# Cached grouped-query attention with a token mixer: half of wq of two heads on partitions 0 to 63, loaded as transfers of four DMA engines

## The chip, the core and the metric

One core of one Trainium2 chip runs the kernel. The metric is device time in microseconds (us), from the start to the end of one execution of the program. Before the change it was 2498.15 us (median of 3 runs, 2498.01 to 2498.72).

## What is computed

Two layers run one after the other on a single new token of two sequences (B = 2, D = 512). Each layer is a block of attention over a cache, and then a token mixer. There are 32 query heads in 8 groups; a group of four shares one head of keys and values, of 32768 positions by 128. Both layers use the same caches and weights. All of it is float32.

```python
def _A_ref(x, k_cache, v_cache, wq, wo):
    q = (x @ wq).reshape(B, Sq, 32, 128).transpose(0, 2, 1, 3)
    k = repeat(k_cache, 4, axis=1)
    v = repeat(v_cache, 4, axis=1)
    p = softmax(einsum("bhqd,bhkd->bhqk", q, k) * 128 ** -0.5)
    o = einsum("bhqk,bhkd->bhqd", p, v)
    return o.transpose(0, 2, 1, 3).reshape(B, Sq, 4096) @ wo
...
x = x + _A_ref(layernorm(x), k_cache, v_cache, wq, wo)
x = x + _B_ref(layernorm(x), w1, b1, w2, b2)
x = x + _A_ref(layernorm(x), k_cache, v_cache, wq, wo)
x = x + _B_ref(layernorm(x), w1, b1, w2, b2)
```

`_B_ref` is a small network (1792 hidden units) across the one token, for each of the 512 channels.

## The kernel before, in words

**Units.** The work is cut into units (layer, b, h): one sequence and one head of keys and values. A unit reads its keys (64 groups of 512 columns, 16 MB) and then its values (64 groups, 16 MB). `k_step` (L350 to L370) multiplies four groups of keys by the four queries into a tile `scores`; `v_step` (L418 to L440) multiplies four groups of values by the exponentials into `acc`. Each such call is a step, and `Order` (L44) lists all steps in the order in which TensorE takes them: the keys of one unit, then the values of the unit before. At the change of layer a few units of both layers are interleaved, since the last sums of the first layer must be complete before a query of the second can be made.

**Memory.** All that is read from DRAM lands in one tile, `mem`, of 106 cells; a cell is 512 floats on 128 partitions (256 KB). `plan_loads` (L120) decides ahead of time, in the order of need, in which cells each load goes and after which step (`begun`) its cells are free. A load is 32 cells (8 MB) of keys or values in most of the run, and smaller around the change of layer and at the end; a piece of weights, wq or wo of one head, is 4 cells (`WCELLS`, 1 MB). There are 240 loads in all. Ten of the cells are left beside three loads of 32, and in most of the run wq of the coming head lies in cells 0 to 3 and wo of the present one in cells 4 to 7.

**Queues.** All these loads are issued by SyncE (the SP queue) in the order of the plan, by `load` (L893): weights at L899, keys and values at L904. The queue is in order: a load that waits for its cells holds back all that come behind it. A transfer of 128 partitions runs on all 16 DMA engines of the core, and each engine works through its own part of the loads in their order. ScalarE issues the two small inputs and the first result.

**Queries.** For each head, `make_q` (L309) forms the queries of both sequences: `wide_products` (L321) multiplies the normalized input by wq. D = 512 lies as four tiles of 128 on the partitions: `xw` (128 x 4 x 32) holds the input, and wq of a head is seen as 128 x 4 x 512. Tile d gives a product of 128 rows into the 32 partitions from 32 d of a tile `bcast` (L325), and `narrow_products` (L332) sums the four and turns them. The tile `xw` is written at the start (`first_input`, L301) and by `change_0` and `change_2` at the change of layer.

Of the kernel before, what the change touches and what calls it, by code (L numbers as in the profile page):

```python
# [8 lines left out]
F32 = mybir.dt.float32  # L9
# [4 lines left out]
P = 128  # L14
G = 512
# [5 lines left out]
WCELLS = 4  # L21
# [17 lines left out]
STEP_US = 1.6  # L39
ASK_Q = 16  # L40
ASK_O = 8


class Order:  # L44
# [75 lines left out]
def plan_loads(order, weights, busy):  # L120
# [13 lines left out]
    queue, array, begun, i = 2.0, 0.0, -1, 0  # L134
# [10 lines left out]
    while i < len(asked) or weights:  # L145
        if weights and (i == len(asked) or weights[0][0] <= asked[i][0]):
            _, name, last = weights.pop(0)
            label, sizes, stays = ("W", name, 0), (WCELLS,), True
        else:
            _, kind, u, g = asked[i]  # L150
            label, stays = (kind, u, g), (kind, u, g) in order.kept
            n = 1
            while (
                i + n < len(asked)
                and asked[i + n][1:] == (kind, u, g + n)
                and (g + n) % HALF
                and ((kind, u, g + n) in order.kept) == stays
            ):
                n += 1
            sizes = [s for s in SIZES if s <= n] or [n]  # L160
            if label in order.sizes:
                sizes = [min(order.sizes[label], n)]
        best = None
        for s in sizes:
            spots = range(CELLS - s + 1)
            found = None
            for a in spots if stays else reversed(spots):
                t = ready(range(a, a + s))
                if t is not None:
                    wait = max(0.0, t + LEAD_US - queue)  # L170
                    key = (wait, t if s == max(SIZES) or label[:2] == ("V", order.last) else 0.0)
                    if found is None or key < found[3]:
                        found = (wait, s, a, key)
            if found is not None and (best is None or found[0] < best[0] - 0.01):
                best = found
            if best is not None and best[0] == 0.0:
                break
        wait, s, a, _ = best
        begun = max(begun, *(last_use[a : a + s]))
        loads.append((label, s, a, begun))  # L180
        queue += wait + s * CELL_US + LOAD_US
        if label[0] == "W":
            last_use[a : a + s] = [last] * s
        else:
            for j in range(s):
                key = (kind, u, g + j)
                for k in (key, order.kept.get(key)):
                    if k is not None:
                        landed[k] = queue + LAND_US
                        last_use[a + j] = step_of[order.back.get(k, k)]  # L190
                if key in order.held:
                    landed[order.held[key]] = queue + LAND_US
            i += s
        while len(done) < len(steps):
            kind, u, g = steps[len(done)]
            keys = [(kind, u, g + j) for j in range(STEP)]
            if any(k not in landed for k in keys):
                break
            array = max(array, *(landed[k] for k in keys)) + STEP_US
            array += busy.get(len(done), 0.0)  # L200
            done.append(array)
# [1 line left out]


@with_exitstack
def gqa_mixer_kernel(ctx: ExitStack, tc: tile.TileContext, x, kt, v, wqo, cols, out):
    nc = tc.nc
    B, D = out.shape
    HKV = wqo.shape[0]
# [2 lines left out]
    DT = D // P  # L212
# [7 lines left out]
    const = ctx.enter_context(tc.tile_pool(name="const", bufs=1))  # L220
# [10 lines left out]
    def cells(a, n):  # L231
        return mem[:, a * G : (a + n) * G]
# [20 lines left out]
    misc = pfix.tile([P, G], F32, name="misc")  # L253
    S = [const.tile([P, G], F32, name=f"S{k}") for k in range(2)]
    xw = const.tile([P, DT, 32], F32, name="xw")
    RAW = B
    xT = {}
    turn = [0, 0, 0]
# [23 lines left out]
    def first_input():  # L282
# [16 lines left out]
        for b in range(B):  # L299
            xT[b] = xcols[:, b, :]  # L300
            nc.vector.tensor_scalar_mul(xw[:, :, b], cen[:, b, :], rs[:, b : b + 1])  # L301

    def row_tile():
        return work.tile([P, D], F32, name="row", bufs=1)

    wq_sb, wo_sb = {}, {}
# [14 lines left out]
    def wide_products(us, wq):  # L321

        q_ps[us] = pfix.tile([P, G], F32, name="bcast")
        for d in range(DT):
            nc.tensor.matmul(q_ps[us][32 * d : 32 * d + 32, :], xw[:, d, :], wq[:, d, :], start=True, stop=True)  # L325

    def narrow_products(us, side):

# [452 lines left out]
    def at(p, f, *args, us=0.0):  # L781
        hooks.setdefault(p, []).append((f, args))
        busy[p] = busy.get(p, 0.0) + us
# [32 lines left out]
    for u in order.units:  # L816
# [35 lines left out]
        e = v_end  # L852
# [24 lines left out]
        at(e + 3, unread, u, G)  # L877
        at(e + 4, change_3, y, us=1.0)
        at(e + 4, unread, u, G // 2)
        assert e + 4 < first["K", y]  # L880

    for x, _, y in order.changes:
# [10 lines left out]
    def load(label, n, a):  # L893
        kind, u, g = label
        if kind == "W":
            part, layer, h = u
            w = D * R
            at_w = 0 if part == "q" else w
            nc.sync.dma_start(cells(a, n), wqo[h][:, at_w : at_w + w])  # L899
            (wq_sb if part == "q" else wo_sb)[layer, h] = cells(a, n).rearrange("p (t c) -> p t c", t=DT)  # L900
            return
        layer, b, h = u
        src = (kt if kind == "K" else v)[b * HKV + h, g // HALF, :, (g % HALF) * G : (g % HALF + n) * G]
        nc.sync.dma_start(cells(a, n), src)  # L904
        for j in range(n):
            at_cell[kind, u, g + j] = a + j
            if (kind, u, g + j) in order.kept:
                at_cell[order.kept[kind, u, g + j]] = a + j
# [6 lines left out]
        load(label, n, a)  # L915
    constants()
    first_input()
    for step in range(3):
        make_q(opening_q, step)
    for p, (kind, u, g) in enumerate(steps):  # L920
# [8 lines left out]
def _layout(A_x, A_k_cache, A_v_cache, A_wq, A_wo, B_w1, B_b1, B_w2, B_b2):  # L929
    import numpy as np  # L930

    B, HKV, SK, DH = A_k_cache.shape
    D = A_x.shape[-1]
    U = B * HKV
    kt = A_k_cache.reshape(U, 2, NG, 32, 2, 2, 8, 2, 2, DH).transpose(0, 1, 9, 4, 7, 8, 2, 5, 6, 3)
    wq = A_wq.reshape(D // P, P, HKV, -1).transpose(2, 1, 0, 3)
    wo = A_wo.reshape(HKV, -1, DH, D).transpose(0, 2, 1, 3)
    w1, b1, w2 = (a.reshape(P, -1) for a in (B_w1, B_b1, B_w2))
    none = np.zeros_like(w2)
    w2z = np.stack([none, w2], axis=2).reshape(P, -1)  # L940
    cols = [w1, b1, w2z, none[:, :1], np.broadcast_to(B_b2.reshape(1, 1), (P, 1))]
    return {
        "x": np.ascontiguousarray(A_x.reshape(B * (D // P), P).T),
        "kt": np.ascontiguousarray(kt).reshape(U, 2, DH, HALF * G),
        "v": A_v_cache.reshape(U, 2, P, HALF * G),
        "wqo": np.concatenate([wq.reshape(HKV, P, -1), wo.reshape(HKV, DH, -1)], axis=2),
        "cols": np.concatenate(cols, axis=1),
    }


_INS = ["x", "kt", "v", "wqo", "cols"]


# [20 lines left out]
```

## Time and profile before

| | |
|---|---|
| median of the runs | 2498.15 us |
| the profiled execution's own time | 2500.69 us |
| its span, first to last instruction | 2498.9 us |
| TensorE busy (matmul) | 1343.6 us, 54% |
| VectorE, ScalarE busy | 211.3 us, 187.4 us |
| bytes read from DRAM | 1063.29 MB, 426 GB/s over the span |
| loads of keys of 8 MB: issue to landing | 49.3 us (median of 51) |
| loads of weights of 1 MB: issue to landing | 38.5 us (median of 28) |

The profiled execution took 2.54 us more than the median of the runs (0.1%); 1.8 us of its time lie outside the span. In the rows of the profile PE is TensorE, DVE VectorE, ACT ScalarE and SPq the queue of SyncE; L899 is line 899 of the kernel before. A row of DMA packets gives their number, their bytes and how many were small; the DMA share is the mean busy share of the 16 DMA engines, and it can pass 1 in a short stretch, since a packet is counted whole where it begins.

### The profile page before, as it was taken

The page shows a single profiled execution, that of the slowest core. Times are in us where ns is not written, and L with a number is a line of the kernel's source. Part 1 is how long each engine was busy: PE and PEld are TensorE (multiplying, and loading weights), DVE is VectorE, ACT ScalarE, POOL GpSimd, SP SyncE. Part 2 cuts the span into 40 slices and gives each one's busy share as a digit, 9 for nine tenths or more (in the row PEclk, how much of TensorE's full clock was granted, in tenths as well). Part 3 has the DMA queues.
Part 4 walks back from the last instruction along what each step waited for, and adds up shares of the span by engine and source line. Part 5 has one row for each costly group of instructions (what it writes and reads, how often), then busy time and mean ns, then how long its engine had stood idle before and what let it go on. Part 6 is the DMA issues. An engine that isn't in the chain of part 4 may idle for free.

```text
span 2498.9 us, 21072 instructions
## 1 busy us (share of the span) xinstructions
PE 1343.6 (54%) x9564; PEld 376.6 (15%) x9564; DVE 211.3 (8%) x600; ACT 187.4 (8%) x582; POOL 5.2 (0%) x18
## 2 busy tenths in 40 slices
PE   3445455545445544556775774555444544464567
PEld 1111111111111111111121221111111111111113
DVE  1000000000000000001110110000000000000012
ACT  0100000000000000001110210000000000000021
POOL 0000000000000000000000000000000000000000
PEclk8777777777777767778887886777777777777788
DMA  9999999999999999999999999999999999999996
GB/s 419 435 435 431 430 435 432 433 427 436 434 431 435 433 431 428 430 432 411 408 429 422 410 429 435 432 430 436 432 434 431 434 436 430 434 427 435 433 432 280
DMA packets 34946, 1064.64 MB, mean 426 GB/s; under 512 B 4133, under 2 KB 4137, under 8 KB 5034
## 3 DMA queue, kind: packets, MB, share of 16 engines
q1 hardware_dynamic: 34568, 1063.27, 99.1%
q8 instruction: 75, 1.23, 0.2%
q14 instruction: 13, 0.11, 0.0%
q10 hardware_dynamic: 290, 0.04, 0.0%
HBM read 1063.29 MB, written 0.00 MB: 426 GB/s over the span
## 4 chain that ended last, share of the span: by engine, by line
DMA 63%; PE 24%; another core or an unknown queue 11%; DVE 1%; issue 0%; ACT 0%; SPq 0%; POOLq 0%; POOL 0%; DVEq 0%; ACTq 0%
DMA mem<-in_v_dram 35%; DMA mem<-in_kt_dram 28%; PE acc L428 13%; PE scores L360 8%; PE misc L332 1%; PE rows L492 0%; PE bcast L325 0%; PE misc L384 0%; PE misc L451 0%; PE misc L657 0%; SPq L904 0%; ACT S L410 0%; PE misc L378 0%; PE misc L471 0%
## 5 line engine op out<-in xcount | busy, mean ns | idle before, releaser
L428 PE MATMUL acc<-mem,S 128*16 128x512 f32 x4080 | 598.9, 719 | 589.9 <-DMA mem<-in_v_dram 581.6
L360 PE MATMUL scores<-mem,qz 128*32 128x512 f32 x4096 | 598.6, 726 | 532.1 <-DMA mem<-in_kt_dram 532.1
L410 ACT ACTIVATE S<-S,neg 128x128 f32<-128x128 f32 x256 | 129.6, 509 | 2213.0 <-DVE S L405 1188.9
L360 PEld LDWEIGHTS scores<-mem,qz 128*32 128x32 f32 x4096 | 142.8, 127 | 915.0 <-issue 819.5
L428 PEld LDWEIGHTS acc<-mem,S 128*16 128x16 f32 x4080 | 127.5, 107 | 904.5 <-issue 818.8
L370 DVE TENSOR_REDUCE mx<-scores 128x1 f32<-128x512 f32 x64 | 44.3, 692 | 797.5 <-PE scores L360 789.7
L405 DVE STREAM_TRANSPOSE S<-scores 128x512 f32<-128x512 f32 x64 | 45.5, 711 | 125.1 <-PE acc L428 125.1
L410 ACT ACTIVATION_READ_ACCUMULATOR S<-S,neg 128x1 f32 x256 | 47.8, 187 | 0.0
L492 PE MATMUL rows<-mem,oz 128*2 128x512 f32 x248 | 44.1, 794 | 0.3 <-DVE oz L481 0.3
L380 DVE TENSOR_REDUCE m<-misc 1x4 f32<-1x128 f32 x32 | 8.9, 279 | 381.4 <-PE misc L378 381.4
L453 DVE RECIPROCAL rl<-misc 128x4 f32<-128x4 f32 x32 | 5.8, 183 | 382.1 <-PE misc L451 382.1
L462 DVE SCALAR_TENSOR_TENSOR row<-acc,quad,row 128x128 f32<-128x128 f32 x96 | 33.7, 351 | 3.4
L460 DVE TENSOR_SCALAR row<-acc,quad 128x128 f32<-128x128 f32 x32 | 11.2, 351 | 172.7 <-PE acc L428 172.7
L481 DVE TENSOR_TENSOR oz<-misc,rl 128x4 f32<-128x4 f32 x32 | 5.2, 162 | 222.8 <-PE misc L471 222.3
L471 PEld LDWEIGHTS misc<-head,row 128*128 128x128 f32 x64 | 14.0, 274 | 52.2 <-issue 38.3
L325 PE MATMUL bcast<-mem,xw 128*32 128x512 f32 x144 | 20.7, 636 | 1.7 <-POOL x_rs L298 1.7
L451 PEld LDWEIGHTS misc<-both,one 128*128 128x128 f32 x64 | 13.8, 271 | 49.7 <-issue 46.8
L471 PE MATMUL misc<-head,row 128*128 128x4 f32 x64 | 16.8, 334 | 7.3 <-DVE row L462 7.3
L332 PEld LDWEIGHTS misc<-selg,row 128*128 128x128 f32 x128 | 17.3, 210 | 19.6 <-issue 10.2
L576 ACT ACTIVATE row<-bcast,bias,scale 128x512 f32<-128x512 f32 x21 | 16.3, 778 | 38.1 <-PE rows L560 16.1
L332 PE MATMUL misc<-selg,row 128*128 128x2 f32 (+1 forms) x128 | 18.7, 268 | 0.8 <-DVE row L317 0.8
L378 PE MATMUL misc<-ident,mxa 128*1 128x128 f32 x64 | 17.0, 360 | 2.0 <-DVE mxa L376 2.0
(137 smaller groups left out, 282.1 us busy)
## 6 DMA issues: line engine op xcount, KB each, us to landing
mem<-in_v_dram SPq DMA_DIRECT2D x13, 4096.0 KB, 25.1
mem<-in_v_dram SPq DMA_DIRECT2D x37, 1024.0 KB, 9.5
mem<-in_kt_dram SPq DMA_DIRECT2D x15, 2048.0 KB, 18.1
mem<-in_kt_dram SPq DMA_DIRECT2D x30, 1024.0 KB, 9.9
mem<-in_wqo_dram SPq DMA_DIRECT2D x28, 1024.0 KB, 38.5
mem<-in_kt_dram SPq DMA_DIRECT2D x6, 4096.0 KB, 29.4
mem<-in_kt_dram SPq DMA_DIRECT2D x2, 6144.0 KB, 25.1
mem<-in_v_dram SPq DMA_DIRECT2D x3, 2048.0 KB, 38.3
```

What stands on the lines that cost most here:

```text
L325: nc.tensor.matmul(q_ps[us][32 * d : 32 * d + 32, :], xw[:, d, :], wq[:, d, :], start=True, stop=True)
L332: nc.tensor.matmul(pt[:, r * n : (r + 1) * n], q_row[us][:, r * DH : (r + 1) * DH], side, start=True, stop=True,)
L360: nc.tensor.matmul(sc_ps[u, half][32 * row : 32 * row + 32, :], qz[:, at : at + 32], cells(at_cell["K", u, g], 1), start=(i == 0), stop=(i ...
L370: nc.vector.tensor_reduce(mx[u][:, half : half + 1], sc_ps[u, half], axis=AX.X, op=ALU.max)
L378: nc.tensor.matmul(pm[:1, :P], mxa, ident, start=True, stop=True)
L405: nc.vector.transpose(S[half], sc_ps[u, half])
L410: nc.scalar.activation(s[:, :, h], s[:, :, h], AF.Exp, bias=neg[u][:, h : h + 1], scale=SCALE, accum_out=lsum[u][:, half, h : h + 1],)
L428: nc.tensor.matmul(acc[32 * row : 32 * row + R * QT, :], S[half][:, col : col + R * QT], vc, start=(g < NG), stop=(g >= quads - NG),)
L462: nc.vector.scalar_tensor_tensor(asb[u], acc[:, t * DH : (t + 1) * DH], quad[:, t : t + 1], asb[u], op0=ALU.mult, op1=ALU.add)
L471: nc.tensor.matmul(po_of[u][:, :R], asb[u], head, start=True, stop=(u != order.last))
L492: nc.tensor.matmul(rows[32 * r : 32 * r + B, :], oT[u][:, 2 * r + 1 - b : 2 * r + 3 - b], wo_of(u)[:, r, :], start=False, stop=(u == order ...
L576: nc.scalar.activation(hid[key, f], px[key], AF.Gelu_apprx_tanh, bias=shift[key][:, f : f + 1], scale=slope[key][:, f : f + 1],)
```

## The change

For two pieces of weights, wq of head 5 for the first layer and wq of head 1 for the second, the second half of the rows (tiles d = 2 and d = 3, 512 KB of the 1 MB) no longer lies on all 128 partitions. It is laid on partitions 0 to 63 alone, in four cells: of each tile first the rows that were on the lower 64 partitions, then those that were on the upper 64. It comes from an input of its own, `low`, in two transfers of 32 partitions, each from four groups of eight rows (8 KB a row) that lie apart in DRAM because a ninth row of each group is left empty. The first half comes as before, in a transfer of 128 partitions and two cells. So such a piece takes 6 cells in place of 4, and three transfers in place of one.

Tiles 2 and 3 then take two products of 64 rows each in place of one of 128. The second of these needs the input of the upper 64 partitions on the lower ones: `lift` copies it into a new tile, `high`, once at the start and once after each of the two changes of the input. The scratch space of software-generated DMAs is halved, which makes room for `high`.

```diff
+LOWER = (("q", 0, 5), ("q", 1, 1))
+LOWER_CELLS = 6
...
-            label, sizes, stays = ("W", name, 0), (WCELLS,), True
+            label, sizes, stays = ("W", name, 0), (LOWER_CELLS if name in LOWER else WCELLS,), True
...
+    high = const.tile([P // 2, DT // 2, 32], F32, name="high")
...
+    def lift():
+
+        nc.vector.tensor_copy(high, xw[P // 2 :, DT // 2 :, :])
...
         for d in range(DT):
-            nc.tensor.matmul(q_ps[us][32 * d : 32 * d + 32, :], xw[:, d, :], wq[:, d, :], start=True, stop=True)
+            to = q_ps[us][32 * d : 32 * d + 32, :]
+            if d < DT // 2 or wq.shape[1] == DT:
+                nc.tensor.matmul(to, xw[:, d, :], wq[:, d, :], start=True, stop=True)
+                continue
+            half, k = P // 2, d - DT // 2
+            nc.tensor.matmul(to, xw[:half, d, :], wq[:half, DT // 2 + 2 * k, :], start=True, stop=False)
+            nc.tensor.matmul(to, high[:, k, :], wq[:half, DT // 2 + 2 * k + 1, :], start=False, stop=True)
...
+        at(e + 7, lift)
...
+            if u in LOWER:
+                nc.sync.dma_start(cells(a, DT // 2), wqo[h][:, : w // 2])
+                for k in range(2):
+                    to = cells(a + DT // 2, DT)[32 * k : 32 * k + 32, :]
+                    nc.sync.dma_start(to, low[LOWER.index(u), k][:, :8, :])
+                wq_sb[layer, h] = cells(a, n).rearrange("p (t c) -> p t c", t=n)
+                return
...
+    lift()
     for step in range(3):
         make_q(opening_q, step)
...
+    low = np.zeros((len(LOWER), 2, 4, 9, 4 * G), np.float32)
+    for i, (_, _, h) in enumerate(LOWER):
+        part = wq[h, :, D // P // 2 :, :].reshape(2, 2, 4, 8, -1, G).transpose(1, 2, 3, 4, 0, 5)
+        low[i, :, :, :8, :] = part.reshape(2, 4, 8, 4 * G)
...
-    nc = bacc.Bacc("TRN2", target_bir_lowering=False, num_devices=1, dynamic_dma_scratch_size=256)
+    nc = bacc.Bacc("TRN2", target_bir_lowering=False, num_devices=1, dynamic_dma_scratch_size=128)
```

The plan of the loads keeps its order. Of the 240 loads six have other cells or another `begun`: each of the two pieces of wq now waits for step 274 (850) in place of 263 (839), because its cells 4 and 5 hold wo of the head before until then; the load of values behind it has step 274 (850) in place of 271 (847), since it may not pass the piece ahead of it in the queue; and the wo behind that lies in cells 6 to 9 in place of 4 to 7.

The SP queue before, around wq of head 5 for the first layer, the first L899 row here (`DMAHW` is a landing that a load waits for, `PE` a matmul):

```order
L904 DMA mem<-in_kt_dram 128x16384 [waits DMAHW5_49,DMAHW2_49,PE_49]
L904 DMA mem<-in_kt_dram 128x16384 [waits DMAHW3_49,PE_49]
L899 DMA mem<-in_wqo_dram 128x2048 [waits DMAHW7_49]
L904 DMA mem<-in_v_dram 128x16384 [waits DMAHW4_49,PE_49]
L899 DMA mem<-in_wqo_dram 128x2048 [waits PE_49]
L904 DMA mem<-in_v_dram 128x16384 [waits DMAHW5_49,PE_49]
```

The same place of the SP queue with the change (L914 and L917 are the new lines of `load`, L925 is the old L904, L920 the old L899):

```order
L925 DMA mem<-in_kt_dram 128x16384 [waits DMAHW5_49,DMAHW2_49,PE_49]
L925 DMA mem<-in_kt_dram 128x16384 [waits DMAHW3_49,PE_49]
L914 DMA mem<-in_wqo_dram 128x1024 [waits DMAHW7_49]
L917 DMA mem<-in_low_dram 32x1x2048 [waits PE_49]
L917 DMA mem<-in_low_dram 32x1x2048
L925 DMA mem<-in_v_dram 128x16384 [waits DMAHW4_49]
L920 DMA mem<-in_wqo_dram 128x2048 [waits PE_49]
L925 DMA mem<-in_v_dram 128x16384 [waits DMAHW5_49,PE_49]
```

The wait for TensorE that stood at the load of wo now stands at the first `low` transfer, ahead of a load of values that had a wait of its own. The place in the second layer, at wq of head 1, reads the same.

TensorE before, in the values of unit (0, 0, 4), where the queries of head 5 are made (L325):

```order
L428 MATMUL acc<-mem,S_91 16x512 x8
L384 MATMUL misc<-m_1760,one 128x4
L428 MATMUL acc<-mem,S_91 16x512 x12
L325 MATMUL bcast<-mem,xw 32x512 x4
L428 MATMUL acc<-mem,S_91 16x512 x4
```

TensorE at the same place with the change (L334, L337 and L338 are the new products, L441 is the old L428):

```order
L441 MATMUL acc<-mem,S_91 16x512 x8
L397 MATMUL misc<-m_1764,one 128x4
L441 MATMUL acc<-mem,S_91 16x512 x12
L334 MATMUL bcast<-mem,xw 32x512 x2
L337 MATMUL bcast<-mem,xw 32x512
L338 MATMUL bcast<-mem,high 32x512
L337 MATMUL bcast<-mem,xw 32x512
L338 MATMUL bcast<-mem,high 32x512
L441 MATMUL acc<-mem,S_91 16x512 x4
```

Six products stand where four did, at the same place among the values; nothing else moves on TensorE.

More of the change, by code (lines that the diff above doesn't have):

```diff
@@ L205, in gqa_mixer_kernel @@
 @with_exitstack
-def gqa_mixer_kernel(ctx: ExitStack, tc: tile.TileContext, x, kt, v, wqo, cols, out):
+def gqa_mixer_kernel(ctx: ExitStack, tc: tile.TileContext, x, kt, v, wqo, low, cols, out):
     nc = tc.nc
@@ L946, in _layout @@
         "wqo": np.concatenate([wq.reshape(HKV, P, -1), wo.reshape(HKV, DH, -1)], axis=2),
+        "low": low,
         "cols": np.concatenate(cols, axis=1),
     }
-_INS = ["x", "kt", "v", "wqo", "cols"]
+_INS = ["x", "kt", "v", "wqo", "low", "cols"]
 def kernel(A_x, A_k_cache, A_v_cache, A_wq, A_wo, B_x, B_w1, B_b1, B_w2, B_b2):
```

## The prediction

> **What bounds the kernel now.** I read the page first, for who is busy throughout.
>
> ```profile
> span 2498.9 us, 21072 instructions
> PE 1343.6 (54%) x9564; PEld 376.6 (15%) x9564; DVE 211.3 (8%) x600; ACT 187.4 (8%) x582; POOL 5.2 (0%) x18
> DMA  9999999999999999999999999999999999999996
> DMA packets 34946, 1064.64 MB, mean 426 GB/s; under 512 B 4133, under 2 KB 4137, under 8 KB 5034
> q1 hardware_dynamic: 34568, 1063.27, 99.1%
> q8 instruction: 75, 1.23, 0.2%
> ```
>
> TensorE is busy for 54%; the sixteen DMA engines are busy for 99% from the first slice to the last but one. The SP queue's packets (q1) take nearly all of that. A stretch of 100 us in the second layer gives their rate (last two columns: DMA share, GB/s):
>
> ```profile
> 1500.00:1600.00 100.00, 51.19 (x316) 12.51 (x320) 5.80 (x15) 4.71 (x18) 0.00 (x0) 0.70 1.01 436
> ```
>
> 436 GB/s on sixteen engines is 27.25 GB/s for each. So the span is the bytes of one engine over its rate, and the question is which engine has most to do. Every load gives each engine the same bytes, yet the engines do not end together. A load ends on each engine with one packet under 512 B: 240 loads on 16 engines make 3840 of the 4133 small packets. Counting small packets in narrow windows therefore shows how many engines end a load there. The DMA view for 702 to 703.8 us, 703.8 to 705.2 and 705.2 to 707.7, shortly before wq of head 5 is due:
>
> ```profile
> DMA packets 22, 0.92 MB, mean 510 GB/s; under 512 B 8, under 2 KB 8, under 8 KB 8
> DMA packets 7, 0.46 MB, mean 328 GB/s; under 512 B 0, under 2 KB 0, under 8 KB 0
> DMA packets 27, 1.25 MB, mean 498 GB/s; under 512 B 8, under 2 KB 8, under 8 KB 8
> ```
>
> Eight engines end that load, then none, then the other eight. The same for 1087.5 to 1089.8, 1089.8 to 1092.2 and 1092.2 to 1094.7 us, just before the small loads of the change of layer:
>
> ```profile
> DMA packets 33, 1.08 MB, mean 470 GB/s; under 512 B 8, under 2 KB 8, under 8 KB 8
> DMA packets 22, 0.92 MB, mean 382 GB/s; under 512 B 0, under 2 KB 0, under 8 KB 0
> DMA packets 30, 1.25 MB, mean 498 GB/s; under 512 B 8, under 2 KB 8, under 8 KB 8
> ```
>
> And for 2435.6 to 2437.8, 2437.8 to 2440.3 and 2440.3 to 2442.4 us, near the end:
>
> ```profile
> DMA packets 29, 0.92 MB, mean 417 GB/s; under 512 B 8, under 2 KB 8, under 8 KB 8
> DMA packets 24, 1.05 MB, mean 419 GB/s; under 512 B 0, under 2 KB 0, under 8 KB 0
> DMA packets 33, 0.82 MB, mean 390 GB/s; under 512 B 8, under 2 KB 8, under 8 KB 8
> ```
>
> The windows are drawn as tight as the counts allow. An early engine's **lead** over the last one is thus 3.9 to 5.7 us at 705 us, 4.9 to 7.2 us at 1090 us and 4.6 to 6.8 us at 2440 us. The end of the loads shows it again:
>
> ```profile
> 2474.00:2475.00 1.00, 1.00 (x16) 0.26 (x8) 0.00 (x0) 0.00 (x0) 0.00 (x0) 1.00 1.03 414
> 2475.00:2476.00 1.00, 1.00 (x13) 0.22 (x6) 0.00 (x0) 0.00 (x0) 0.00 (x0) 1.00 0.60 248
> 2477.00:2478.00 1.00, 0.64 (x8) 0.25 (x12) 0.00 (x0) 0.00 (x0) 0.00 (x0) 1.00 0.47 197
> 2480.00:2481.00 1.00, 1.00 (x35) 0.72 (x26) 0.78 (x3) 0.00 (x0) 0.00 (x0) 1.00 0.43 164
> 2481.00:2482.00 1.00, 1.00 (x26) 0.65 (x26) 0.00 (x0) 0.00 (x0) 0.00 (x0) 1.00 0.08 29
> ```
>
> From 2475 to 2481 us half of the engines are dry and the other half still load the last values. **The eight late engines set the time.** A likely reason is in the q8 row: 75 instruction packets, 16 KB each, took 0.2% of sixteen spans, 80 us or 1.07 us each. On eight engines that is 10 us each, near the 4.9 to 7.2 and 4.6 to 6.8 us of lead that the two layers show.
>
> **The change, part by part.** *Bytes.* A piece of wq gave each engine 1 MB / 16 = 64 KB. Now its 128-partition half gives each 32 KB, and the two `low` transfers give four engines 2 x 64 KB more. At 27.25 GB/s the other twelve save 32 KB, **1.20 us**, per piece, and the four gain 96 KB, **3.61 us**. [...] The trace of before shows no such transfer beside the loads.
>
> If the four are early engines, a piece costs them 3.61 + 1.20 = 4.81 us of lead. In the first layer a lead of 3.9 to 5.7 us falls to between -0.9 and +0.9 us and grows back to between 0.1 and 2.4 us at 1090 us, as its rise from 705 to 1090 us shows: the late eight still end last, 1.20 us sooner. In the second, 4.6 to 6.8 us falls to between -0.2 and 2.0 us: the last engine ends 1.0 to 1.20 us sooner. Together -2.2 to -2.4 us.
>
> *Speed of the `low` transfers.* No row has four engines writing 32 partitions. From below, their packets run at 27.25 GB/s like all others; faster is excluded, since all engines run at one rate here. From above, the nearest slow packet is q8's, 16 KB in 1.07 us, 15.3 GB/s: then 128 KB take 8.5 us in place of 4.8 and a piece costs the four 3.7 us more. I take the lower end, because in shape (8 KB rows from DRAM to `mem`) they are q1's packets, and keep the other for the range.
>
> *The SP queue.* These rows show the issues around the two pieces.
>
> ```profile
> 679.50 0.33 SPq L904 DMA_DIRECT2D mem<-in_kt_dram  x1
> 679.89 0.41 SPq L899 DMA_DIRECT2D mem<-in_wqo_dram  x1
> 699.12 0.33 SPq L904 DMA_DIRECT2D mem<-in_v_dram  x1
> 713.07 0.33 SPq L899 DMA_DIRECT2D mem<-in_wqo_dram  x1
> ...
> 2032.05 1.45 SPq L899 DMA_DIRECT2D mem<-in_wqo_dram  x1
> ...
> 2066.94 0.33 SPq L899 DMA_DIRECT2D mem<-in_wqo_dram  x1
> ```
>
> ```profile
> mem<-in_kt_dram SPq DMA_DIRECT2D x51, 49.3
> SPq L899 <- PE rows L492: 118.5, 8, 15.3
> ```
>
> The wait for the matmuls of L492 moves from wo to the first `low` transfer, so that the `low` transfers go out at 713.07 us in place of 679.89, and the load of values behind them at about 714.3 (three issues of 0.4 us) in place of 699.12; in the second layer 2066.94 for 2032.05. The keys issued at 679.50 land 49.3 us later by the row, at 728.8 us on the last engine, on the early ones up to 5.7 us before, 723.1 us. So the engines have 9 us of work when the values are issued, and the delay costs nothing. It would cost if that wait were over 9 us longer; at first the early engines alone would go dry. Two more issues per piece, 0.8 us of the SP queue, have the same cover.
>
> *TensorE and VectorE.*
>
> ```profile
> 749.49 3.39 PE L428 MATMUL acc<-mem,S 128*16 128x512 f32 x16 [12.61 <-DMA mem<-in_v_dram]
> 757.61 1.04 PE L325 MATMUL bcast<-mem,xw 128*32 128x512 f32 x8
> L325 PE MATMUL bcast<-mem,xw 128*32 128x512 f32 x144 | 20.7, 636 | 1.7 <-POOL x_rs L298 1.7
> L346 DVE COPY qz<-misc 128x4 f32<-128x4 f32 x32 | 3.9, 158 | 46.2 <-PE misc L332 46.2
> L462 DVE SCALAR_TENSOR_TENSOR row<-acc,quad,row 128x128 f32<-128x128 f32 x96 | 33.7, 351 | 3.4
> ```
>
> Four products are eight instructions and took 1.04 us; two more products add four instructions, between 0.5 us (in proportion) and 2.5 us (one after the other, 636 ns each). TensorE had just waited 12.61 us for values and waits again for the next ones: hidden, and 0.5 to 2.5 us per piece without that cover. It needs the piece at 757.6 us. The values behind it in the queue land before that (749.49 us), so a piece up to 8 us later still holds back nothing. `lift` is a copy of 64 x 64, between the 158 ns of 4 columns and the 351 ns of 128, three times; VectorE is busy for 8%. At the start it stands ahead of the first queries, at most 0.35 us on a path which the first keys hide (49.3 us from issue to landing by their row). The other scratch size moves nothing in these queues.
>
> *Sum.* The profiled execution took 2500.69 us, 2.54 us above the median of the runs. 2500.69 - 2.3 = 2498.4 us for such an execution, and **2498.15 - 2.3 = 2495.9 us** for the median.
>
> **The rivals.** *B, the four engines write where others write.* Partitions 0 to 31 also belong to loads that other engines run beside them. At the q8 rate a piece costs the four 4.81 + 3.7 = 8.5 us of lead against 4.9 to 7.2 and 4.6 to 6.8 us: they end 1.3 to 3.6 and 1.7 to 3.9 us after the relieved eight, that is 0.1 to 2.4 and 0.5 to 2.7 us later than before. Middle sum +2.9 us: 2501.0 us (2498.8 to 2503.3). For it: the full stretch above has each engine at one rate, as a limit on each engine's own path would give. Against it: early and late engines, 5 us apart and so on different loads, run side by side at that rate. [...]
>
> *C, slower: some of the four are late engines.* The rows count engines and do not name them. A late one has no lead: it takes 3.61 us more per piece, and the time is 2498.15 + 7.2 = 2505.4 us. It decides from the point where one of the four has less than 3.61 us of lead; with one in the first layer only it is about +2.4 us. [...]
>
> *D, nothing is moved, or it is given back.* If the `low` transfers ran on all sixteen engines, the bytes would be as before: 2498.2 us. If the change of layer hid the first layer's gain, 2497.0 us.
>
> **How the numbers follow.** Forecast (A) 0.42, its own range 2495.3 to 2497; B 0.33; C 0.15; D 0.10. What a measurement here can tell from no change is about 0.2%, 5.0 us. No case reaches that gain: faster 0.03, for what I do not see. Slower holds nearly all of C and the end of B: 0.23. Within 0.2%: 0.74. The range from 2494.9 to 2505.6 us takes in all four at these prices; what it leaves out are B or C at a higher price.
>
> **What would show it.** Right: in the last stage the DMA share falls to a half at about the same time as before, and to nothing some 2.3 us sooner; the small packets near 1090 and 2440 us stand 1.2 us and 2.4 us earlier in their late group, and four of the early group have moved next to it. B: the `low` transfers take far over 5 us, and a few engines end after the eight. C: a late group with up to 7 us more. Wrong in the cover: DMA share under 0.9 near 713 to 730 us or 2067 to 2085 us, or a wait of TensorE at the products of L334 to L338.

## The result, and the profile after

| | before | after |
|---|---|---|
| median of the runs | 2498.55 us (2498.01 to 2499.27, 7 runs) | 2507.07 us (2505.53 to 2507.75, 7 runs) |
| profiled execution, span | 2500.69 us, 2498.9 us | 2507.75 us, 2506.0 us |

The change makes the kernel slower: the ratio is 1.0033, with a 95% interval of 1.0021 to 1.0045. The forecast was 2495.9 us, and the time lies above the whole range. The page of the kernel after, the lines that answer to those of before:

```profile
span 2506.0 us, 21095 instructions
PE 1349.6 (54%) x9572; PEld 378.7 (15%) x9572; DVE 212.0 (8%) x603; ACT 187.5 (7%) x582; POOL 5.1 (0%) x18
...
DMA  9999999999999999999999999999999999999996
GB/s 419 434 433 432 433 433 431 432 430 439 433 392 435 433 434 432 426 436 412 418 423 425 416 429 434 433 432 433 435 431 429 432 433 404 434 430 434 430 430 280
DMA packets 35090, 1064.64 MB, mean 425 GB/s; under 512 B 4149, under 2 KB 4153, under 8 KB 5306
...
q1 hardware_dynamic: 34712, 1063.27, 99.1%
```

The bytes are the same and the DMA engines are still 99% busy. But two slices of 62.65 us stand out in the GB/s row: 392 in the twelfth and 404 in the thirty-fourth. The same row of before:

```profile
GB/s 419 435 435 431 430 435 432 433 427 436 434 431 435 433 431 428 430 432 411 408 429 422 410 429 435 432 430 436 432 434 431 434 436 430 434 427 435 433 432 280
```

It has 431 and 430 there. 39 GB/s over 62.65 us are 2.4 MB, and 26 are 1.6 MB; at 432 GB/s that is 5.7 and 3.8 us. These slices hold the two pieces with `low`. Closer in, the stretches of 10 us around them in the kernel after (last two columns: DMA share, GB/s):

```profile
714.00:724.00 10.00, 4.10 (x40) 0.96 (x32) 0.69 (x1) 0.00 (x0) 0.00 (x0) 0.90 1.00 415
724.00:734.00 10.00, 4.38 (x24) 1.26 (x28) 0.00 (x0) 0.00 (x0) 0.00 (x0) 0.50 1.03 267
734.00:744.00 10.00, 5.65 (x48) 1.41 (x40) 0.85 (x2) 0.00 (x0) 0.00 (x0) 0.84 0.96 415
2069.00:2079.00 10.00, 4.24 (x40) 0.96 (x32) 0.69 (x1) 0.00 (x0) 0.00 (x0) 0.90 1.06 434
2079.00:2089.00 10.00, 4.48 (x32) 1.40 (x36) 0.00 (x0) 0.00 (x0) 0.00 (x0) 0.58 0.98 263
2089.00:2099.00 10.00, 3.95 (x40) 0.97 (x32) 0.85 (x2) 0.00 (x0) 0.00 (x0) 0.93 0.98 426
```

and in the kernel before:

```profile
724.00:734.00 10.00, 6.35 (x40) 1.87 (x44) 0.00 (x0) 0.00 (x0) 0.00 (x0) 0.60 1.06 457
...
2079.00:2089.00 10.00, 8.35 (x64) 2.42 (x64) 0.00 (x0) 0.00 (x0) 0.00 (x0) 0.76 1.02 441
```

For some 10 us, twice, the core loads 267 and 263 GB/s in place of 457 and 441, **and the DMA share stays at 1**. The share says that packets are in flight, not how fast they move. The trace keeps a record of every packet, with its bytes and its duration. Between 715 and 745 us, 37 of 152 packets of 64 KB took a mean of 3.67 us, where the median of the run is 2.42 us; the 64 packets of 8 KB, which are `low`, took 553 ns on the mean, where the median is 313 ns. At 729.5 us nine packets of 64 KB are in flight at once, of 4.5 to 4.6 us each, beside four of 8 KB (465 to 542 ns) and three of 4 KB from the first half of the piece (240 to 262 ns, where the first ones of that transfer took 159). That makes sixteen. So all engines were held up, not only the four that write `low`.

The SP queue did what was forecast (`low` at 713.07 us and the values at about 714.3 us there); the second column is the duration:

```profile
679.69 0.41 SPq L914 DMA_DIRECT2D mem<-in_wqo_dram  x1
712.99 1.49 SPq L917 DMA_DIRECT2D mem<-in_low_dram  x2
714.52 0.44 SPq L925 DMA_DIRECT2D mem<-in_v_dram  x1
```

At the end, where nothing is loaded any more, the granted clock of TensorE matters. The kernel after, 2484 to 2488, 2488 to 2490 and 2490 to 2494 us (last three columns: granted clock, DMA share, GB/s):

```profile
2484.00:2488.00 4.00, 4.00 (x78) 2.37 (x70) 1.41 (x4) 0.00 (x0) 0.00 (x0) 1.00 0.48 181
2488.00:2490.00 2.00, 1.09 (x18) 0.51 (x18) 0.46 (x2) 0.00 (x0) 0.00 (x0) 1.00 0.00 0
2490.00:2494.00 4.00, 4.00 (x32) 1.92 (x25) 1.33 (x4) 0.38 (x1) 0.00 (x0) 0.57 0.00 0
```

The clock falls to 0.57 in the middle of the last token mixer. From the end of the last product with values (L441) to the issue of `out` it took 18.35 us, and 16.91 us in before. This is one execution; its time lies 0.7 us above the median.

### The profile page after: what moved, and what is told of

It reads as the page before. It is cut to its first block, busy times and chain, and to the rows that moved or that the text cites. A ratio compares the mean times of both kernels' runs of the same rounds, so it can differ in the third digit from the quotient of the medians.

```text
span 2506.0 us, 21095 instructions
## 1 busy us (share of the span) xinstructions
PE 1349.6 (54%) x9572; PEld 378.7 (15%) x9572; DVE 212.0 (8%) x603; ACT 187.5 (7%) x582; POOL 5.1 (0%) x18
## 2 busy tenths in 40 slices
DMA packets 35090, 1064.64 MB, mean 425 GB/s; under 512 B 4149, under 2 KB 4153, under 8 KB 5306
## 4 chain that ended last, share of the span: by engine, by line
DMA 63%; PE 25%; another core or an unknown queue 10%; DVE 1%; ACT 1%; issue 0%; SPq 0%; POOLq 0%; POOL 0%; ACTq 0%; DVEq 0%
DMA mem<-in_v_dram 35%; DMA mem<-in_kt_dram 28%; PE acc L441 13%; PE scores L373 8%; PE rows L505 1%; PE misc L345 1%; PE bcast L334 0%; PE misc L397 0%; PE misc L484 0%; PE misc L464 0%; PE misc L670 0%; DVE row L475 0%; ACT S L423 0%; ACT mem L781 0%
## 5 line engine op out<-in xcount | busy, mean ns | idle before, releaser
L441 PE MATMUL acc<-mem,S 128*16 128x512 f32 x4080 | 602.3, 724 | 582.2 <-DMA mem<-in_v_dram 574.0
L441 PEld LDWEIGHTS acc<-mem,S 128*16 128x16 f32 x4080 | 128.7, 108 | 900.3 <-issue 818.2
L334 PE MATMUL bcast<-mem,xw 128*32 128x512 f32 x136 | 20.6, 638 | 1.7 <-POOL x_rs L301 1.7
L484 PE MATMUL misc<-head,row 128*128 128x4 f32 x64 | 16.8, 333 | 7.3 <-DVE row L475 7.3
L345 PEld LDWEIGHTS misc<-selg,row 128*128 128x128 f32 x128 | 17.1, 208 | 20.3 <-issue 9.8
```

The costliest lines, as they stand in the source:

```text
L334: nc.tensor.matmul(to, xw[:, d, :], wq[:, d, :], start=True, stop=True)
L345: nc.tensor.matmul(pt[:, r * n : (r + 1) * n], q_row[us][:, r * DH : (r + 1) * DH], side, start=True, stop=True,)
L441: nc.tensor.matmul(acc[32 * row : 32 * row + R * QT, :], S[half][:, col : col + R * QT], vc, start=(g < NG), stop=(g >= quads - NG),)
L484: nc.tensor.matmul(po_of[u][:, :R], asb[u], head, start=True, stop=(u != order.last))
```

## The experiments

All times are medians; a ratio is that to the kernel before in the same comparison, with its 95% interval. A measured GB/s is that of 724 to 734 and of 2079 to 2089 us. In the diffs, lines that lay out `low` in DRAM are left out. In this first group the kernel before stands at 2498.01 us (e1 to e4) and 2498.07 us (e5 to e8) in the same comparisons. The records name neither the engine of a packet nor the partitions it writes. "Own" and "foreign" in the names of the runs are therefore what theory P below supposes, and the pair e3 and e4 is its test: "own" stands for partitions 0 to 15 and 32 to 47 (e3, 462 and 439 GB/s) and, in fours over eight engines, for 0 to 63 (e5, 461 and 432), "foreign" for 16 to 31 and 48 to 63 (e4, 352 and 347). In the kernel after each `low` transfer ran on four engines: its page has 16 more packets under 512 B than that of before (4149 against 4133), four for each, and at 729.5 us four of the 8 KB packets are in flight. That e1 runs on sixteen engines and e2, e5 and e8 on eight is my assumption; the sums in the last section fit it.

### What holds up the engines

Theory P: writing on partitions that another engine serves at the time. Rivals: S, the spaced groups or the source in DRAM; F, the bytes that the few engines gain, as in the prediction's rival C.

**e1_sixteen.** `low` without gaps, one transfer of 64 partitions, taken to run on sixteen engines, so that each has its bytes of before.

```diff
+                nc.sync.dma_start(cells(a + DT // 2, DT)[: P // 2, :], low[LOWER.index(u)])
```

> The same layout (half of the piece on partitions 0 to 63, six cells, six products), but the 512 KB lie without gaps and come in one transfer of 64 partitions, which divides over all sixteen engines. Theory P (each few partitions have a path of their own; an engine that writes on another's partitions shares that path, and while it does all engines are held up): sixteen engines then share the paths of the lower half, a dip in GB/s remains, shorter; 2499 to 2504 us. Theory S (the rows of the new input are slow to read from DRAM): the dip is as in the changed kernel, about 2507 us. Theory F (only the bytes that four engines have to carry count): each engine has the bytes of the kernel before, no dip, 2498.5 us.

Measured 2510.13 us (ratio 1.0050, 1.0033 to 1.0067); 247 and 288 GB/s. On sixteen engines none has more bytes than before, so F, which forecast no dip, falls, and the groups are gone as well. P forecast a dip, but at most 2504 us: its price was too low.

**e2_eight.** Eight spaced groups of eight rows, one transfer of 64 partitions, taken to run on eight engines.

```diff
+                nc.sync.dma_start(cells(a + DT // 2, DT)[: P // 2, :], low[LOWER.index(u)][:, :8, :])
```

> The same layout, but one transfer from eight spaced groups of eight rows, so on eight engines. Theory P: still rows on others' partitions, a dip of GB/s as in the changed kernel or somewhat shorter, 2500 to 2507 us. Theory S: 2507 us. Theory F: each of the eight carries only 32 KB more per piece than before, and they are early engines: 2496 us.

Measured 2512.56 us (1.0058, 1.0043 to 1.0073); 257 and 259 GB/s. More engines for the same rows don't help, and the time is again above what P forecast (2500 to 2507 us).

**e3_own and e4_foreign.** Half of the rows of `low` are left out (the products take what the cells held). Two transfers of four groups of four rows go to partitions 0 to 15 and 32 to 47 (e3) or to 16 to 31 and 48 to 63 (e4). P supposes that the first are the four engines' own, and that others serve the second.

```diff
+                    at = 32 * k + 0     # e4: + 16
+                    to = cells(a + DT // 2, DT)[at : at + 16, :]
+                    nc.sync.dma_start(to, low[LOWER.index(u), k][:, :4, :])
```

> [...] The products read what lies in the cells. Theory P: no dip (over 420 GB/s around 724 to 734 us and 2079 to 2089 us), 2496 us, since twelve engines have 32 KB less per piece and four 32 KB more. Theory S: a dip of half the length, about 2502 us. Theory F: 2496 us without a dip.

> [...] Theory P: a dip of about half the length of the changed kernel's, some 2 us per piece: about 2500 us, 4 us above the run with own partitions. Theory S: as that run, 2502 us both. Theory F: 2496 us both.

Measured 2497.81 us for e3 (1.0000, 0.9991 to 1.0009) and 2503.40 us for e4 (1.0022, 1.0012 to 1.0031). e3:

```profile
724.00:734.00 10.00, 6.68 (x49) 2.01 (x53) 0.00 (x0) 0.00 (x0) 0.00 (x0) 0.68 1.08 462
...
2079.00:2089.00 10.00, 8.22 (x64) 2.23 (x56) 0.85 (x2) 0.00 (x0) 0.00 (x0) 0.85 1.01 439
```

e4:

```profile
724.00:734.00 10.00, 3.58 (x24) 1.08 (x28) 0.00 (x0) 0.00 (x0) 0.00 (x0) 0.54 1.03 352
...
2079.00:2089.00 10.00, 5.47 (x32) 1.57 (x36) 0.00 (x0) 0.00 (x0) 0.00 (x0) 0.53 0.90 347
```

Same number of engines, same bytes, same groups, same form of source: only the partitions differ, and e4 is 5.6 us slower, with the dip that e3 doesn't have. P stands, S and F fall. (Both lie some 2 us above P's 2496 and 2500 us; where these 2 us come from is the next group's question.)

**e6_shift.** As e3, on partitions 4 to 19 and 36 to 51: three of the four groups lie where another group lay in e3, the fourth where one lay in e4.

```diff
+                    at = 32 * k + 4
```

> [...] Theory P1, what counts is two engines at once on one path: only one of the four meets a streaming engine, a short dip, 2498.5 to 2501 us. Theory P2, any write away from an engine's own partitions is slow and holds up the rest: as the run with foreign partitions, 2503 us.

Measured 2499.90 us (1.0006, 0.9997 to 1.0015); 382 and 412 GB/s. A small dip, 2.1 us above e3 where e4 is 5.6 us above it. In the terms of P, writing elsewhere is cheaper where the owner is itself away. That speaks for two writers meeting, which no record shows.

**e5_eight_own and e8_four_pieces.** The whole of `low` in two transfers of eight groups of four rows, which go on by fours where e3 left off, so that they fill partitions 0 to 63; e8 does it to four pieces.

```diff
                     to = cells(a + DT // 2, DT)[32 * k : 32 * k + 32, :]
-                    nc.sync.dma_start(to, low[LOWER.index(u), k][:, :8, :])
+                    nc.sync.dma_start(to, low[LOWER.index(u), k][:, :4, :])
```

> [...] Theory P (shared paths hold up all engines): no dip, 2496 to 2498 us, 9 to 11 us under the changed kernel. Its rival, that transfers of fewer than sixteen engines or of spaced rows are slow as such: a dip as in the run with eight engines and groups of eight rows, 2507 to 2513 us.

> As the run of eight engines on own partitions, but for four pieces: wq of heads 3 and 5 in the first layer, 3 and 1 in the second. If the eight late engines set the time, they save 1.2 us per piece: 2493.4 us, 2.4 us under the same with two pieces. If the time does not follow them: 2498 us.

Measured 2502.58 us (1.0016, 1.0008 to 1.0025) and 2505.27 us (1.0028, 1.0017 to 1.0040); 461 and 432 GB/s in e5, so no dip. Yet both are slower than before and than forecast (2496 to 2498 us for e5, 2493.4 or 2498 us for e8). Two causes were left: the eight engines that write `low`, with 32 KB more per piece, and something that the other kernels carry as well. The landings of one load near the end tell of the first: as in the prediction, a packet under 512 B marks an engine that ends the load. e5, 2433.5 to 2435, 2435 to 2441.5 and 2441.5 to 2443.2 us:

```profile
DMA packets 13, 0.66 MB, mean 437 GB/s; under 512 B 2, under 2 KB 2, under 8 KB 2
DMA packets 81, 2.79 MB, mean 429 GB/s; under 512 B 12, under 2 KB 12, under 8 KB 12
DMA packets 20, 0.59 MB, mean 347 GB/s; under 512 B 2, under 2 KB 2, under 8 KB 2
```

2, 12 and 2 engines, where before has 8 and 8. The counts fit when, of the eight that write `low`, six are early and meet the relieved late ones in the middle, and two are late and now end last. So rival C holds for two of these eight; the sizes of e5 and e8 bear it out below. For the four of the change it doesn't: e3, 2431 to 2433, 2433 to 2437 and 2437 to 2439.5 us:

```profile
DMA packets 16, 0.66 MB, mean 328 GB/s; under 512 B 4, under 2 KB 4, under 8 KB 4
DMA packets 45, 1.90 MB, mean 475 GB/s; under 512 B 4, under 2 KB 4, under 8 KB 4
DMA packets 36, 0.92 MB, mean 367 GB/s; under 512 B 8, under 2 KB 8, under 8 KB 8
```

Four untouched early engines, the four of the change moved towards the end, and eight late ones, still last.

**e7_none.** No `low` transfer at all (the products take what the cells held): 32 KB less per piece on every engine.

```diff
-                for k in range(2):
-                    to = cells(a + DT // 2, DT)[32 * k : 32 * k + 32, :]
-                    nc.sync.dma_start(to, low[LOWER.index(u), k][:, :8, :])
```

> Leaves out the transfers of the new input altogether; the products read what lies in the cells. All else of the change stays: the six cells, the later issue, the extra products, the copies. If these cost nothing, all engines have 32 KB less per piece: 2495.6 us and no dip. If the wait that moved to an earlier place of the queue, or the products, cost time: 2499 us and more.

Measured 2498.23 us (1.0001, 0.9992 to 1.0010). The relief of 2.4 us doesn't show, and here not even the few engines gain bytes. Either a relief is given back, or another part of the change costs as much.

### What ate the gain

**e9_plan and e12_plan_four.** The kernel after with bytes as before: the second half of the rows comes on 128 partitions, into the last two of the six cells (the products read cells with other data). e12 has four such pieces.

```diff
+                nc.sync.dma_start(cells(a + WCELLS, DT // 2), wqo[h][:, w // 2 : w])
```

**e10_relief and e11_relief_all.** The kernel before with the second half of the rows not loaded, in the same two pieces, or in twelve.

```diff
+            if u in (("q", 0, 5), ("q", 1, 1)):     # e11: part == "q" and (layer or h > 1)
+                nc.sync.dma_start(cells(a, DT // 2), wqo[h][:, : w // 2])
+            else:
...
```

> The kernel after, but the second half of wq of the two pieces comes as a transfer of 128 partitions from its old place, into the last two of the six cells: bytes per engine as before, and the six cells, the moved wait, lift, the extra products and the small scratch as after. The products read cells that hold other data, so the output isn't the reference's. Theory G (what bounds is the bytes of the engines, and these other parts are hidden, as the prediction has it): 2498.1 us. Theory K (these other parts cost about the 2.4 us by which the kernel without the transfers missed its gain): 2500.0 to 2500.8 us. Theory H (a relief of two pieces is given back whatever the plan): 2498.1 us as well; it is told from G by the next kernel.

> The kernel before, with the second half of wq of the same two pieces not loaded (the products take what the cells held): 32 KB less for each of the sixteen engines per piece, and nothing else changed. G and K: 2 x 1.20 us less, 2495.6 to 2495.8 us. H (the relief is given back): 2497.6 to 2498.3 us.

> As the kernel of e10, with the second half not loaded in twelve pieces of wq (six in each layer). The sum of the prediction says 12 x 1.20 = 14.4 us less, 2483.6 us, if the bytes of the engines set the time everywhere. If the relief is given back in part by something that follows the order of the work, it is less than half of that: 2491 us or more.

> The kernel of e9 with four pieces (wq of heads 3 and 5 for the first layer, 3 and 1 for the second). G and H: 2498.1 us. K: twice the cost of e9, 2502 to 2503.5 us. Beside it stands the kernel of eight own engines with four pieces (2505.3 us): what lies between the two is what 32 KB more on the lower eight engines and 32 KB less on the upper eight do; if the lower eight are the late ones, that is 4 x 1.20 = 4.8 us, if they are the early ones it is 0 or less.

| | us (runs) | ratio to before, 2498.13 us | expected |
|---|---|---|---|
| e9 | 2500.26 (11) | 1.0009 (1.0000 to 1.0018) | G 2498.1, K 2500.0 to 2500.8 |
| e10 | 2495.71 (11) | 0.9990 (0.9981 to 0.9999) | G, K 2495.6 to 2495.8 |
| e11 | 2483.87 (4) | 0.9943 (0.9929 to 0.9956) | 2483.6 |
| e12 | 2500.29 (11) | 1.0008 (0.9999 to 1.0017) | G 2498.1, K 2502 to 2503.5 |

The relief works as computed: -2.42 us for two pieces, -14.26 us for twelve, 1.19 us each. And the kernel after carries 2.1 us from elsewhere, whether two pieces are changed or four (the interval of e9 just reaches 1 and that of e12 includes it, but the lowest runs of both, 2500.13 and 2500.10, lie above the highest of 27 of before, 2499.39); K is right on the cost and wrong that it goes by the piece. e5 and e8 are now explained: they stand 2.3 and 5.0 us above e9 and e12, and 32 KB more per piece on the two late engines make 2 x 1.20 and 4 x 1.20 us.

**e13 to e16.** One part each: the halved scratch space alone (e13); that with `high` and `lift` (e14); six cells, the moved wait and the split transfer (e15, all computed as in before); all of e9 but `high`, `lift` and the scratch space (e16, whose added products take other rows of `xw`).

```diff
-    nc = bacc.Bacc("TRN2", target_bir_lowering=False, num_devices=1, dynamic_dma_scratch_size=256)
+    nc = bacc.Bacc("TRN2", target_bir_lowering=False, num_devices=1, dynamic_dma_scratch_size=128)
```

(e13; e14 adds the tile and the three calls as the change has them; e15 adds `LOWER`, `LOWER_CELLS` and the two transfers of e9; e16 takes the first two out of e9.)

> The kernel before with the scratch space of software DMAs halved, nothing else. Theory K1 (the scratch space is the fixed cost): 2500.0 to 2500.4 us. K2 (lift), K3 (the plan and the moved wait) and K4 (none of them by itself): 2498.1 us.

> The kernel before with the scratch space halved, the tile high and the three calls of lift, whose result nothing reads. K1 and K2: 2500.0 to 2500.4 us, told apart by e13. K3 and K4: 2498.1 us.

> The kernel before with six cells for the two pieces: the first half of the rows in the first two, the second half in the last two, each a transfer of 128 partitions, so that the wait for TensorE moves from wo to the second of them; the products read these cells. Scratch space as before, no high, no lift, no low. K3 (plan and wait): 2500.0 to 2500.4 us. K1, K2 and K4: 2498.1 us.

> The kernel of e9 without high and lift and with the scratch space of before: the two more products per piece take rows of xw, so the output isn't the reference's. K1 and K2: 2498.1 us. K3: 2500.0 to 2500.4 us. K4 (only all together, or any shift of the code): something else again, told from the others by e13 to e15 all at 2498.1.

Beside 2498.39 us for before: 2500.62 (e13), 2500.40 (e14), 2498.18 (e15), 2498.39 (e16), 11 runs each; the intervals of e13 and e14 just reach 1 (0.9999 and 1.0000), but their lowest runs, 2500.08 and 2500.07, lie above the highest of 33 runs of before, 2499.41. The halved scratch space is the whole of it.

**e17_back and e18_512.** In the built programs `mem` begins at byte 416 of its partitions before and at byte 288 after: halving the scratch space moves it by 128 bytes. e17 keeps it halved and puts 128 unused bytes ahead of `mem` (416 again); e18 keeps it as before and puts 96 bytes there (512).

```diff
+    const.tile([P, 32], F32, name="pad")     # e18: [P, 24]
     mem = const.tile([P, CELLS * G], F32, name="mem")
```

> The kernel before with the scratch space halved and an unused tile of 128 bytes ahead of mem, so that mem and all behind it lie where they lay before. Theory L (the place of mem in its partitions costs the 2.2 us): 2498.2 us. Theory S (the size of the scratch space itself): 2500.4 us.

> The kernel before with its scratch space and an unused tile of 96 bytes ahead of mem, so that mem begins at byte 512 in place of 416. Theory S: 2498.2 us. Theory L: another time than 2498.2; where rows that begin on a multiple of 512 bytes are the better ones, below it, 2496 us or less, which would be a version faster than both kernels.

(S is here the size of the scratch space.) Beside 2498.48 us for before: e17 2497.83 us (0.9998, 0.9989 to 1.0007, 11 runs), e18 **2490.01 us** (0.9965, 0.9952 to 0.9977, 5 runs). It is the place of `mem`, not the scratch space, and e18 is faster than both kernels, by 8.5 and 17.1 us. The page of e18:

```profile
span 2487.8 us, 21072 instructions
...
DMA packets 34946, 1064.64 MB, mean 428 GB/s; under 512 B 4133, under 2 KB 4137, under 8 KB 5034
...
q1 hardware_dynamic: 34568, 1063.27, 99.2%
```

Same packets, same bytes, 99.2% of a shorter span: each packet is a little shorter. From the packet records of whole runs, means:

| `mem` at byte | kernel | 64 KB packet | 16 KB packet | q1 packets, us per engine | median us |
|---|---|---|---|---|---|
| 288 | e13 | 2425.5 ns | 618.3 ns | 2476.3 | 2500.62 |
| 416 | e17 | 2424.4 ns | 617.0 ns | 2474.6 | 2497.83 |
| 512 | e18 | 2420.7 ns | 615.3 ns | 2467.1 | 2490.01 |

An engine has some 2160 packets in q1; 3.5 ns less on each are the 7.6 us between the last two rows. Between the first two the packets give 1.7 us of the 2.2 us that e13 stands above before; the rest isn't in them.

## Why the prediction was wrong

From the median of before in the comparison with after: 2498.55 - 2.4 (relief, e10) + 2.2 (`mem` at byte 288, e13) = 2498.3 us; the remaining 8.7 us up to 2507.07 are the hold-up. The packet records bear this out. From 713 to 747 and from 2066 to 2098 us, the q1 packets that were over 5% longer than usual (2421, 313 and 159 ns for 64, 8 and 4 KB) took 4.4 and 4.1 us per engine more than at the usual length, 8.6 us together. The same sum is 5.8 us in e4 (measured 5.6 us above e3), 9.8 us in e1, 9.5 us in e2, and 0.1 us in e3 and e5. The slices' 5.7 + 3.8 us are rougher, and the 1.4 us of the clock belong to the profiled execution, which is the slowest of the seven.

- **Bytes, right.** That a `low` transfer gives its bytes to four engines, the source of the 2 x 64 KB, nothing ahead of the prediction shows; the 16 small packets more in the kernel after (4149 against 4133), four for each of the four transfers, do. 1.20 us per piece for relieved engines; the runs gave 1.21 and 1.19. The bytes set the time (e11), and those of the eight late engines: e3 with more on four early ones costs nothing beside its 2.2 us, e5 and e8 with more on two late ones cost 2.3 and 5.0 us.
- **The four are early, right.** At the load of 2440 us, the kernel after has 4, 0 and 12 small packets in 2440.5 to 2442.5, 2443 to 2445.5 and 2445.5 to 2449 us: the four have moved next to the late eight, as the prediction said they would. C didn't happen; e3, with 64 KB more on these four than on the rest in each piece, stands where the relief and the 2.2 us put it. This was partly luck: no row of before tells which side the four are on, and of the eight that write `low` in e5 two are late.

```profile
DMA packets 20, 0.85 MB, mean 426 GB/s; under 512 B 4, under 2 KB 4, under 8 KB 4
DMA packets 20, 1.05 MB, mean 419 GB/s; under 512 B 0, under 2 KB 0, under 8 KB 0
DMA packets 53, 1.41 MB, mean 403 GB/s; under 512 B 12, under 2 KB 12, under 8 KB 12
```

- **Speed of the `low` transfers, the step that failed.** "I take the lower end, because in shape (8 KB rows from DRAM to `mem`) they are q1's packets". Their shape is q1's, their place isn't. 8 KB took 553 ns on the mean, 14.8 GB/s, close to the upper end of 15.3. But that alone would have cost what B says, 0.1 to 2.7 us per piece. What no case had is that **the others slow down as well**. B had the place right and the payer wrong: it charged the price to the lead of four engines, and the runs charge it to all, 8.6 us. B's first mark (`low` far over 5 us: 16 packets of 553 ns on each engine, 8.8 us) came; its second (a few engines end after the eight) doesn't show, since the last twelve end within 3.5 us of each other. What all sixteen share there, no run here tells.
- **"The other scratch size moves nothing in these queues", the second step that failed.** It moves no instruction, and it moves `mem` by 128 bytes, 2.2 us. That is nearly the whole gain: without the dips the change would have gained 0.2 us.
- **SP queue, TensorE, VectorE, right.** The moved wait, the six cells and the added products cost nothing: e15 and e16 stand at 2498.18 and 2498.39 us. e14 is no slower than e13, so `lift` costs nothing. The products and `lift` in the kernel after (mean ns in the middle):

```profile
L337 PE MATMUL bcast<-mem,xw 64*32 64x512 f32 x8 | 2.1, 601 | 0.0
L338 PE MATMUL bcast<-mem,high 64*32 64x512 f32 x8 | 2.1, 589 | 0.0
L308 DVE COPY high<-xw 64x64 f32<-64x64 f32 x3 | 0.6, 190 | 0.1
```

190 ns lie in the bounds of 158 and 351.
- **The range.** Its upper part was B or C. Where the price of a shared place is unknown, the bound "only the writers pay" was itself a choice, and the range had no case without it.
- **"Wrong in the cover: DMA share under 0.9."** The mark stayed silent, with a share of 1.03 and 0.98 in the two dips, since it looks at the wrong column. GB/s was the column to name. Its other half, a wait of TensorE at the new products, didn't come: 0.0 us of idle time stand at L337 and L338 above.

## What to carry to other kernels

Before loading a part of the partitions with a part of the engines, try it on several sets of partitions beside the loads that run there: here, with the same bytes on as many engines, groups of four rows on partitions 0 to 15 and 32 to 47 cost no more than their bytes (e3), and on 16 to 31 and 48 to 63 they held up what was loading, 5.6 us more (e4). When DMA engines are the bound, read GB/s beside the DMA share, and look at the byte at which the loaded tile begins as at any other tuning value; 96 unused bytes ahead of it gained 8.5 us, where the change was to gain 2.3. And an edit that only makes room moves tiles: try it alone.

## What the runs showed of the hardware

- **Writes at other places.** Two pieces of 256 KB at the places of e4 cost 5.6 us against those of e3. For the rest an estimate: if the same group in order goes to the same engine in all these runs, an engine's place is where its groups of four rows lie in e5 (0.1 us in the packets over length), and 448 KB per piece lie off it in the kernel after (about 8.7 us) and in e2 (10.0 us against e5; only partitions 0 to 3 and 60 to 63 are in place): 10 to 11 us per MB in all three. Two don't follow it: e1 with sixteen writers (256 KB off place if each engine takes four rows, 9.9 us against e9), and e6, where the writers go to each other's places (2.1 us against e3).
- **How many engines take a transfer.** With bytes per engine as before, the 2.2 us of e13 and the 9.8 us over length in its packets e1 comes to 2498.01 + 2.2 + 9.8 = 2510.0 us, and 2510.13 was measured; two late engines with 32 KB more per piece would make it 2512.4 us. In e2 they do: 2498.01 + 2.2 + 2.4 + 9.5 = 2512.1 us, and 2512.56 was measured. So e1 fits sixteen engines, and e2 the eight of e5 (2, 12 and 2 landings there in place of 8 and 8).
- **The first byte of a row.** Byte 512 saved 3.5 ns per packet against byte 416. Of the three places tried, 512 is the fastest (2490.01 us), then 416 (2497.83), then 288 (2500.62). The reason is open, and so is what other places would give.
- **The granted clock at the end.** Where the last products meet a low clock they take longer. The same two groups in e9, whose clock is 1.00 there (0.70 and 0.59 us), and in after, where it is 0.5 (1.22 and 1.06 us):

```profile
2484.57 0.70 PE L733 MATMUL bcast<-mem,selg 128*128 128x256 f32 x2
...
2485.10 0.59 PE L733 MATMUL held<-mem,selg 128*128 128x256 f32 x2
```

```profile
2491.38 1.22 PE L733 MATMUL bcast<-mem,selg 128*128 128x256 f32 x2
...
2492.39 1.06 PE L733 MATMUL held<-mem,selg 128*128 128x256 f32 x2
```

  From the last product with values to `out` the profiles had 16.8 to 17.0 us in most kernels, 17.5 in e3 and e7, and 18.3 in after, e6 and e13. In these five the trace has one stretch of 3.4 us at a granted clock of 0.5 there, and none in the others. The load is over by then, so this goes into the time of that execution whole. What lowers the clock is open.
- **Not settled.** The profiled execution of before (2500.69 us) has 2476.9 us of q1 packets per engine, where e17 with `mem` at the same byte has 2474.6; 2.3 of its 2.5 us above the median are thus in its DMA packets, nearly all of them between 1100 and 1400 us, around the change of layer. What made them longer in that execution is unknown. Why eight engines are late was not tested either; that the instruction packets fall on them is an estimate. Whether `low` at the places of e3 with `mem` at byte 512 would gain both ways wasn't tried.
